# Last keys' scores beside the value products of the pairs before, row sums on another PSUM bank, and a first tile in fp32

## The chip, the cores and the metric

The kernel runs on one core of a Trainium2 chip. The metric is the device time of one execution in microseconds (us). Five engines take part: TensorE (PE; its weight loads are shown as PEld), VectorE (DVE), ScalarE (ACT), GpSimd (POOL) and the queue SP, which issues all DMAs. Each runs its own instructions in the order in which the program holds them, and waits where an instruction needs what another engine makes.

## What is computed

The reference chains three blocks over a batch of 4 with 448 positions. The inputs q and k are scaled by 8.

```python
# 1: attention with capped scores, 12 heads of 64
scores = cap * np.tanh((q @ k.T / 8) / cap)          # q, k, v: (4, 12, 448, 64), cap = 30
attn = np.exp(scores - scores.max(-1))
x = (attn / (attn.sum(-1) + 1e-9)) @ v               # heads joined: (4, 448, 768)
# 2: feed-forward with a gated convolution
h = np.maximum(x @ w_in, 0.0)                        # (4, 448, 1024)
c = conv over positions of h, 3 taps per channel
x = (h * sigmoid(c)) @ w_out                         # (4, 448, 768)
# 3: four experts of causal attention (width 64), the top two per position weighted
for e in range(4):
    q, k, v = x @ wq[e], x @ wk[e], x @ wv[e]
    out += weight[e] * (causal_softmax(q @ k.T / 8) @ v @ wo[e])
```

## The kernel before

The program is written as a list of operations (class `Plan`), each with its engine; `ORDER`, a table of numbers, then says in which order they are issued, and `SWAP` which copies stand on DVE instead of ACT or the other way round. Nothing is decided at run time.

**Block 1** works on pairs of heads, g = 0 to 23, six for each batch; rows 0 to 63 of the array hold one head of the pair and rows 64 to 127 the other. The 448 keys are three tiles of 128 keys and 64 last keys.
- `load(g)` fetches q and k. The first six pairs (`JOINT = 6`, batch 0) come as one padded block `kq` of 960 columns, in which the 64 last keys of both heads are laid out as a tile of 128 columns with zeros. Later pairs come as two transfers from `qk_more`.
- `split(g)` makes a high and a low part of q and k (type fp32r). A score is then three products: high times high, high times low, low times high.
- `qk(g, c)`: for c = 0 to 2 the scores of 128 keys, six products in 64x128 tiles, into two PSUM banks; then tanh and exp on ACT (operands called fm<-ps and fm<-fm in the profile). For c = 3 (`NK`) the last keys: in batch 0 three products of 128 rows for each pair, later, for two pairs at once, four plain fp32 products in 64x64 tiles (each fp32 product is two records) into banks 5 and 6.
- `pv(g)`: the value product in fp32, 128x64 tiles. In batch 0 eight products (sixteen records), the last keys among them; later six (twelve records), and after the second pair of a double four 64x64 products for the last keys of both. It ends in bank 7 in batch 0, later in bank 1 (even pairs) or 2 (odd pairs), from which ACT or DVE copies it (`OSB`).
- `sums(g)`: after every second pair the row sums of the exponentials, eight products in 128x32 tiles; batch 0 gathers them in bank 0 and adds four products for the last keys, later batches use bank 2, from which DVE's `gather` adds them up.
- `recip(b)` and `x_unit(b, i)`: the reciprocal of a batch's sums, spread by products and multiplied into the values, which DVE then splits.

**Block 2**: `wi_prep` decodes w_in (stored as 64-bit floats) on DVE and ACT, quarter by quarter, while batches 0 and 1 run; `f_unit(b, f, half)` is nine products of x with w_in, in 128x128 tiles. The first of them, of batch 0 (tag `f0_0`), is the point that the steps below call F. These products are the filler between the attention of the next batch. Results go to DRAM. `fold_mm` multiplies w_out with the weights of block 3, and **block 3** follows from 318 us or so to the end (`v_unit`, `proj_unit`, `scores2`, `tr2`, `pv2`, `wo_unit`).

All matrix products are recorded at line 373, transposes at 377, ACT's work at 313, DVE's at 321, DMAs at 382. A product in another tiling than the one before it (64x128, 64x64, 128x64, 128x32, 128x128) is a change of tiling.

Of the kernel before, what the change touches and what calls it, by code (L numbers as in the profile page):

```python
# [1417 lines left out]
```

## Time and profile before

| what | value |
| --- | --- |
| median of 3 runs | 539.81 us (539.22 to 539.86) |
| profiled execution | 539.78 us, its span 538.1 us |
| PE, PEld busy | 528.6 us (98%), 416.0 us (77%) |
| DVE, ACT busy | 457.4 us (85%), 364.8 us (68%) |
| chain that ended last | PE 88%, DVE 6%, ACT 4% |
| DMA | 64.03 MB, mean 119 GB/s |

An engine's busy time is the union of its instructions; a duration shown is longer than the step to the next instruction where the two overlap. The span runs from the first to the last record of the execution. A row of the timeline has a start, a duration, the engine, the operands, the number of instructions merged in it, and in brackets the idle time before it with what ended it.

### The profile page before, as it was taken

What the parts mean: (1) busy time and instruction counts of PE and PEld (TensorE: products, weight loads), DVE (VectorE), ACT (ScalarE), POOL (GpSimd) and SP (SyncE); (2) the same over time, 40 slices, a digit from 0 to 9 for tenths busy, and PEclk for the clock granted to TensorE, in tenths of its full rate; (3) what the DMA queues carried; (4) which work ended last, traced back from release to release, by engine and by line L of the source; (5) the groups of instructions that cost most, each with busy time, mean ns of one, the idle gap of its engine ahead of it and who ended that gap; (6) DMA issues with size and microseconds to landing.
All of it is one profiled execution on the core that took longest, in us unless ns stands there. A gap on an engine that the chain in (4) does not pass through costs nothing.

```text
span 538.1 us, 9349 instructions
## 1 busy us (share of the span) xinstructions
PE 528.6 (98%) x3304; PEld 416.0 (77%) x3304; DVE 457.4 (85%) x1070; ACT 364.8 (68%) x666; POOL 17.4 (3%) x71
## 2 busy tenths in 40 slices
PE   8899999999999999999999999999999999999997
PEld 6455777455656767569999999999978998999886
DVE  7999998988878886999868999798998988964772
ACT  6999967878985867943324656647857884853672
POOL 8000000000000000000000003000000000000000
PEclk9999999999999999999999999999999999999999
DMA  7464444521512251136657441245235134404413
GB/s 237 144 184 148 136 138 160 149 87 54 158 49 81 93 156 56 54 107 188 163 196 223 118 133 27 78 131 151 77 92 152 58 94 132 123 2 105 122 71 138
DMA packets 41535, 64.03 MB, mean 119 GB/s; under 512 B 7184, under 2 KB 30224, under 8 KB 41488
## 3 DMA queue, kind: packets, MB, share of 16 engines
q1 hardware_dynamic: 41488, 63.44, 39.7%
q8 instruction: 26, 0.43, 0.3%
q14 instruction: 21, 0.17, 0.1%
HBM read 41.13 MB, written 12.85 MB: 100 GB/s over the span
## 4 chain that ended last, share of the span: by engine, by line
PE 88%; DVE 6%; ACT 4%; issue 1%; DMA 1%; ACTq 0%; DVEq 0%
PE ps L373 85%; ACT fm L313 4%; DVE fm L321 3%; DVE rm L321 3%; PE ps L377 3%; DMA fm<-first 1%; ACT rm L313 0%; DVE ps L321 0%; ACTq L313 0%; DVEq L321 0%
## 5 line engine op out<-in xcount | busy, mean ns | idle before, releaser
L373 PE MATMUL ps<-rm 128*128 128x448 f32 (+5 forms) x2352 | 409.6, 352 | 2.4 <-ACT fm L313 1.3
L373 PEld LDWEIGHTS ps<-rm 128*128 128x128 f32 (+1 forms) x2352 | 357.4, 188 | 56.5 <-issue 14.7
L313 ACT ACTIVATE fm<-fm 128x448 f32<-128x448 f32 (+8 forms) x219 | 163.4, 770 | 46.8 <-DVE fm L321 35.5
L321 DVE SCALAR_TENSOR_TENSOR fm<-fm 128x448 f32<-128x448 f32 (+5 forms) x240 | 148.1, 634 | 7.0 <-ACT fm L313 4.5
L313 ACT ACTIVATE fm<-ps,fm 128x896 f32<-128x896 f32 (+4 forms) x143 | 109.9, 788 | 36.8 <-DVE fm L321 18.4
L373 PE MATMUL ps<-fm 128*64 128x448 f32 (+7 forms) x824 | 114.0, 469 | 3.2 <-ACT fm L313 1.8
L321 DVE TENSOR_TENSOR rm<-fm,rm 128x448 fp32r<-128x448 f32 (+4 forms) x152 | 89.4, 603 | 8.7 <-ACT rm L313 7.6
L373 PEld LDWEIGHTS ps<-fm 128*64 128x64 f32 (+3 forms) x824 | 44.6, 133 | 60.3 <-issue 41.4
L313 ACT ACTIVATE fm<-ps 128x448 f32<-128x448 f32 (+4 forms) x113 | 49.9, 463 | 46.3 <-PE ps L373 33.7
L321 DVE TENSOR_TENSOR fm<-fm 64x448 f32<-64x448 f32 (+6 forms) x112 | 60.7, 550 | 7.3 <-ACT fm L313 6.4
L313 ACT ACTIVATE rm<-fm 128x448 fp32r<-128x448 f32 (+6 forms) x83 | 42.7, 535 | 24.4 <-DVE fm L321 15.2
L321 DVE TENSOR_SCALAR fm<-fm 128x256 int32<-128x256 int32 (+11 forms) x138 | 43.2, 320 | 7.3 <-ACT fm L313 6.2
L321 DVE CAST rm<-fm 128x448 fp32r<-128x448 f32 (+6 forms) x77 | 30.8, 403 | 3.8 <-DMA fm<-first 2.6
L321 DVE COPY fm<-ps 128x448 f32<-128x448 f32 (+5 forms) x43 | 18.3, 433 | 12.9 <-PE ps L373 7.1
L313 ACT ACTIVATE rm<-ps 128x386 fp32r<-128x386 f32 (+3 forms) x39 | 16.1, 422 | 15.1 <-PE ps L373 12.8
L321 DVE TENSOR_REDUCE fm<-ps 128x1 f32<-128x128 f32 (+3 forms) x56 | 24.7, 448 | 0.6
L321 DVE TENSOR_TENSOR ps<-ps,fm 128x128 f32<-128x128 f32 (+1 forms) x56 | 15.3, 285 | 10.3 <-PE ps L373 8.8
L321 DVE TENSOR_TENSOR fm<-fm,ps 128x448 f32<-128x448 f32 (+1 forms) x30 | 16.5, 573 | 5.5 <-PE ps L373 5.1
L321 DVE TENSOR_TENSOR rm<-ps,rm 128x386 fp32r<-128x386 f32 (+1 forms) x32 | 18.7, 587 | 2.9 <-ACT rm L313 2.7
L396 POOL MEMSET fm<- 64x3 f32 (+12 forms) x43 | 7.2, 200 | 368.0 <-DVE fm L321 367.1
L377 PE MATMUL ps<-fm 128*128 128x128 f32 x128 | 17.4, 274 | 0.3 <-ACT fm L313 0.3
L377 PEld LDWEIGHTS ps<-fm 128*128 128x128 f32 x128 | 14.7, 140 | 1.6 <-ACT fm L313 0.5
(22 smaller groups left out, 71.6 us busy)
## 6 DMA issues: line engine op xcount, KB each, us to landing
g_dram<-fm SPq DMA_DIRECT2D x32, 224.0 KB, 3.2
fm<-g_dram SPq DMA_DIRECT2D x32, 224.0 KB, 2.9
fm<-w_in SPq DMA_DIRECT2D x24, 256.0 KB, 3.4
fm<-woT SPq DMA_DIRECT2D x16, 384.0 KB, 3.4
out<-fm SPq DMA_DIRECT2D x23, 224.0 KB, 2.3
fm<-v SPq DMA_DIRECT2D x24, 192.0 KB, 3.5
fm<-qk_more SPq DMA_DIRECT2D x18, 256.0 KB, 3.5
rm<-rm SPq DMA_DIRECT2D x32, 128.0 KB, 2.3
```

The lines of the kernel that those rows point to most:

```text
L313: return self.add("act", cost, [lambda: self.nc.scalar.activation(out, in_, func, **kw)], [out] + more, [in_] + ptr)
L321: return self.add("dve", cost, [lambda: f(out, *ins, **kw)], [out], aps)
L373: self.nc.tensor.matmul(out, a, b, start=start, stop=stop, **kw))
L377: calls = [lambda o=o, i=i, d=d: self.nc.tensor.transpose(o, i, d) for o, i, d in parts]
L396: self.add("pool", cost, [lambda: f(out, *ins, **kw)], [out], [x for x in list(ins) + [kw.get("in_")] if hasattr(x, "ap")])
```

## The change

Four things are changed together, and the whole table of issue is new.
- All 24 pairs are loaded and split alike: q with its 64 last keys (512 columns) and the 384 other keys as two transfers; `JOINT` and the padded block are gone. For the very first pair q and the first 128 keys come first, then the other keys, then the last keys.
- `last_keys(g)`: the four fp32 products for the last keys of pairs g and g + 1, their tanh and exp, in all batches, placed by their due time (`QQ_L`) beside the value products of the two pairs before; the value product of batch 0 takes the form that the later batches had, in banks 7 and 2.
- `sums` uses bank 3 instead of bank 2 in batches 1 to 3; it may be recorded ahead of later work (`sums_now`).
- The very first tile of scores (g = 0, c = 0) is two plain fp32 products of unsplit q and k instead of six products of split ones.

The diff, cut to its core; what is left out are the two tables and the data layout on the host.

```diff
-JOINT = 6
+QQ_L = 1.0
...
     def load(g):
-        if g >= JOINT:
-            RAW[g] = RQT.next(), RKT.next()
-            for t, c in zip(RAW[g], (slice(0, QS_N), slice(QS_N, QS_N + KW))):
-                pl.load(t, qk_more[g - JOINT][:, c])
+        q, k = RQT.next(), RKT.next()
+        if g:
+            RAW[g] = q[:, :S], k, q[:, S:]
+            for t, c in ((q, slice(0, QS_N)), (k, slice(QS_N, QS_N + KW))):
+                pl.load(t, kq[g][:, c])
             return
-        RAW[g] = RAWT.next()
-        if g:
-            pl.load(RAW[g], kq[g])
-        else:
-            pl.load(fm.take(1 + HEAD, raw_at - 1), first)
-            pl.load(RAW[g][:, HEAD:], kq[0][:, HEAD:])
+
+        r, n = fm.take(S + KW, raw_at), HEAD - S
+        RAW[0] = r[:, :S], r[:, S:], fm.take(KR, later + 3 * WI_C)
+        pl.load(fm.take(1 + HEAD, raw_at - 1), first)
+        pl.load(r[:, HEAD:], kq[0][:, QS_N + n:])
+        pl.load(RAW[0][2], kq[0][:, S:QS_N])
...
+    def last_keys(g):
+
+        parts, ps = [], banks[:, 5:7]
+        for i, y in enumerate((g, g + 1)):
+            q, _, k = RAW[y]
+            for j, (a, _) in enumerate(sides):
+                parts.append((ps[halves(y)[j], i, :S], k[a], q[a], True, True))
+            PS[y] = cut(P2B, 2)[:, i]
+        pl.mm(parts)
+        p = cut(P2B, 2)
+        pl.act(p, ps[:, :, :S], AF.Tanh, scale=tsc)
+        pl.act(p, p, AF.Exp, scale=cap_in)
...
-        f = 1 if c == 2 and g >= JOINT else (3, 5, 1)[(4 * g + c) % 3] if g < NP else 3 + 2 * (c % 2)
+        f = (3, 5, 1)[c]
...
+        if g == c == 0:
+            parts = [(o, RAW[0][1][a, :128], RAW[0][0][a], True, True) for o, a in lanes]
...
-        if not whole and g >= JOINT:
-
-            if not g % 2:
-                return
-            parts, ps = [], banks[:, 5:7]
-            for i, y in enumerate((g - 1, g)):
-                r = RAW.pop(y)[0]
-                for j, (a, _) in enumerate(sides):
-                    parts.append((ps[halves(y)[j], i, :S], r[a, S:], r[a, :S], True, True))
-            pl.mm(parts)
...
     def pv(g):
-        ps = PB[g % 2] if g >= JOINT else bank(7)
+        ps = PB[g % 2] if g >= NP else bank((7, 2)[g % 2])
         O[g] = ps
-        gs = (g,) if g < JOINT else (g - 1, g) if g % 2 else ()
+        gs = (g - 1, g) if g % 2 else ()
...
-        more, sb = b in DIRECT, bank(2 if b else 0)
+        more, sb = b in DIRECT, bank(3 if b else 0)
...
             if g < NG:
+                if g % 2 == 0 and s == (2 if g else NK):
+                    at(q - QQ_L, "qq%d_%d" % divmod(g, NP))
+                    last_keys(g)
```

What the new order makes of this is shown at three places. First TensorE at the very start. In these rows the size is that of the output; ps<-fm 128x128 are idle products that keep the engine at work, ps<-rm the products of split parts, ps<-fm 64x448 value products and 64x64 groups, one row for each product. Before:

```order
L373 MATMUL ps<-fm 128x128 x7
L373 MATMUL ps<-rm 128x448 x12
L373 MATMUL ps<-fm 128x128
L373 MATMUL ps<-rm 128x448 x3
L373 MATMUL ps<-fm 128x128 x3
L373 MATMUL ps<-rm 128x448 x6
L373 MATMUL ps<-fm 128x128
L373 MATMUL ps<-rm 128x448 x21
L373 MATMUL ps<-fm 64x448 x8
```

The same place after the change, up to the first value products:

```order
L374 MATMUL ps<-fm 128x128 x5
L374 MATMUL ps<-fm 128x448 x2
L374 MATMUL ps<-rm 128x448 x12
L374 MATMUL ps<-fm 128x128 x5
L374 MATMUL ps<-fm 64x448 x4
L374 MATMUL ps<-fm 128x128
L374 MATMUL ps<-rm 128x448 x6
L374 MATMUL ps<-fm 128x128
L374 MATMUL ps<-rm 128x448 x24
L374 MATMUL ps<-fm 64x448 x20
```

The two plain products of the first tile stand ahead of all split ones, the last keys of the first two pairs among the idle products, and the value products of two pairs in one run of twenty with a group of last keys.

Second, TensorE in batch 1, around the row sums (32x224) of its second and third double. Before:

```order
L373 MATMUL ps<-fm 64x448 x12
L373 MATMUL ps<-rm 128x448 x12
L373 MATMUL ps<-fm 64x448 x4
L373 MATMUL ps<-fm 32x224 x8
L373 MATMUL ps<-fm 64x448 x4
L373 MATMUL ps<-rm 128x448 x33
L373 MATMUL ps<-fm 64x448 x16
L373 MATMUL ps<-fm 32x224 x8
L373 MATMUL ps<-rm 128x448 x15
```

The same stretch after the change:

```order
L374 MATMUL ps<-fm 64x448 x20
L374 MATMUL ps<-fm 32x224 x8
L374 MATMUL ps<-rm 128x448 x54
L374 MATMUL ps<-fm 64x448 x12
L374 MATMUL ps<-fm 32x224 x8
L374 MATMUL ps<-fm 64x448 x8
L374 MATMUL ps<-rm 128x448 x15
```

The last keys (x4 on their own before) stand in one run with the value products and their shared part, and scores no longer stand between them.

Third, VectorE from the reciprocal of batch 0's sums on, the way to F. ps in an operand is a product that is read from PSUM, rm a split part that is written; 128x256 is w_in. Before:

```order
L321 RECIPROCAL fm<-ps 128x224
L321 SCALAR_TENSOR_TENSOR fm<-fm 128x256
L321 CAST rm<-fm 128x224
L321 SCALAR_TENSOR_TENSOR rm<-rm,fm 128x224
L321 SCALAR_TENSOR_TENSOR fm<-fm 128x256
L321 TENSOR_TENSOR rm<-fm,rm 128x256
L321 TENSOR_TENSOR fm<-fm,ps 128x448 x2
L321 CAST rm<-fm 128x448
L321 TENSOR_TENSOR fm<-fm,ps 128x448
L321 CAST rm<-fm 128x448
L321 TENSOR_TENSOR fm<-fm,ps 128x448
L321 TENSOR_TENSOR rm<-fm,rm 128x256
```

After the change:

```order
L322 RECIPROCAL fm<-ps 128x224
L322 TENSOR_TENSOR rm<-fm,rm 128x448 x2
L322 CAST rm<-fm 128x224
L322 TENSOR_TENSOR rm<-fm,rm 128x256
L322 SCALAR_TENSOR_TENSOR rm<-rm,fm 128x224
L322 SCALAR_TENSOR_TENSOR fm<-fm 128x256
L322 TENSOR_SCALAR fm<-fm 128x256
L322 TENSOR_TENSOR fm<-fm,ps 128x448 x2
L322 SCALAR_TENSOR_TENSOR fm<-fm 128x256 x3
L322 TENSOR_TENSOR fm<-fm,ps 128x448 x2
L322 SCALAR_TENSOR_TENSOR fm<-fm 128x896
L322 CAST rm<-fm 128x448
```

Between the reciprocal and the split that F needs stand more decoding of w_in, two splits of the next pairs' q and a sum over 896 columns. Up to that split they are 33 instructions, where 19 stood before.

## Rows read from the trace of the kernel before

**Rows 1.** Page: the span, and the engines' busy time, share and instructions.

```profile
span 538.1 us, 9349 instructions
PE 528.6 (98%) x3304; PEld 416.0 (77%) x3304; DVE 457.4 (85%) x1070; ACT 364.8 (68%) x666; POOL 17.4 (3%) x71
```

**Rows 2.** Stretches: length, busy time of each engine, granted clock, DMA share, GB/s.

```profile
0.00:57.00 57.00, 53.65 (x370) 30.37 (x370) 52.92 (x115) 51.51 (x58) 12.93 (x57) 1.00 0.56 173
57.00:126.00 69.00, 67.29 (x440) 44.51 (x436) 62.65 (x136) 53.27 (x72) 0.00 (x0) 1.00 0.41 126
126.00:340.00 214.00, 214.00 (x1301) 167.42 (x1294) 186.66 (x346) 137.11 (x201) 4.35 (x12) 1.00 0.39 117
```

**Rows 3.** Timeline of TensorE at F, the first product with w_in.

```profile
59.92 0.47 PE L373 MATMUL ps<-rm 128*128 128x448 f32 x1
```

**Rows 4.** TensorE's waits (us, times, longest), and its timeline at two row sums.

```profile
PE ps L373 <- ACT fm L313: 3.1, 6, 1.1
...
PE ps L373 <- DMA fm<-v: 0.3, 1, 0.3
...
103.11 1.88 PE L373 MATMUL ps<-fm 128*32 128x224 f32 x24 [0.75 <-ACT fm L313]
...
116.11 1.15 PE L373 MATMUL ps<-fm 128*32 128x224 f32 x16 [0.69 <-ACT fm L313]
```

**Rows 5.** Timeline of TensorE in batch 0: last keys, row sums, a value product.

```profile
35.95 0.86 PE L373 MATMUL ps<-rm 128*128 128x448 f32 x3
36.75 3.98 PE L373 MATMUL ps<-fm 128*64 128x224 f32 x24
...
42.88 3.23 PE L373 MATMUL ps<-fm 128*64 128x448 f32 x16
```

**Rows 6.** Timeline of TensorE in batches 1 to 3: steps with and without changes.

```profile
78.30 2.09 PE L373 MATMUL ps<-rm 128*128 128x448 f32 x9
80.31 0.61 PE L373 MATMUL ps<-fm 64*64 64x448 f32 x4
...
139.90 0.98 PE L373 MATMUL ps<-fm 64*64 64x448 f32 x8
140.81 5.12 PE L373 MATMUL ps<-rm 64*128 64x448 f32 x26
...
261.89 18.40 PE L373 MATMUL ps<-rm 128*128 128x448 f32 x90
```

**Rows 7.** Timelines of TensorE and ScalarE in the opening, and ScalarE ahead of F.

```profile
1.11 3.35 PE L373 MATMUL ps<-fm 128*128 128x128 f32 x14 [1.11 <-DVE fm L577]
...
8.34 0.83 PE L373 MATMUL ps<-fm 128*128 128x128 f32 x6
...
6.57 2.60 ACT L313 ACTIVATE fm<-ps,fm 128x896 f32<-128x896 f32 x3 [0.53 <-PE ps L373]
...
58.16 0.58 ACT L313 ACTIVATE rm<-fm 128x448 fp32r<-128x448 f32 x1
```

**Rows 8.** Groups by form, TensorE: count, busy us, mean ns of one, idle before.

```profile
L373 PE MATMUL ps<-fm 64*64 64x448 f32 x144 | 17.5, 560 | 0.4 <-ACT fm L313 0.4
```

**Rows 9.** Timeline of VectorE from 38 us to F.

```profile
38.42 1.15 DVE L321 SCALAR_TENSOR_TENSOR fm<-fm 128x896 f32<-128x896 f32 x1
...
49.46 0.28 DVE L321 TENSOR_SCALAR fm<-fm 128x256 f32<-128x256 f32 x1
49.66 0.41 DVE L321 SCALAR_TENSOR_TENSOR fm<-fm 128x256 int32<-128x256 int32 x1
...
50.73 1.55 DVE L321 RECIPROCAL fm<-ps 128x224 f32<-128x224 f32 x1
...
56.31 0.62 DVE L321 TENSOR_TENSOR fm<-fm,ps 128x448 f32<-128x448 f32 x1
56.84 0.42 DVE L321 TENSOR_TENSOR rm<-fm,rm 128x256 fp32r<-128x256 f32 x1
...
59.28 0.62 DVE L321 TENSOR_TENSOR rm<-fm,rm 128x448 fp32r<-128x448 f32 x1
```

More of the change, by code (lines that the diff above doesn't have):

```diff
@@ L27 @@
 SG = S + 64
-KQ = S + SG
 QS_N = S + KR
@@ L56 @@
 LV_0 = 4
+WI_C = 256
 WI_0 = 0.5
@@ L453, with chain_kernel @@
 F_WORDS = 19712
-def chain_kernel(tc, first, kq, qk_more, v, w_in, conv_w, woT, wqkv, wo, out):
+def chain_kernel(tc, first, kq, v, w_in, conv_w, woT, wqkv, wo, out):
     nc = tc.nc
@@ L504, in chain_kernel @@
     cap_in, eps, tsc = capt[:, 63:], capt[:, 4:5], capt[:, 5:6]
-    RAWT = fm.ring(2, KQ)
-    fm.take(3 * QS_N + 2 * KW - 2 * KQ)
+    fm.take(3 * QS_N + 2 * KW)
     RQT = Ring([fm.take(QS_N, raw_at + n) for n in (0, QS_N + 2 * KW, 2 * QS_N + 2 * KW)])
@@ L528, in chain_kernel @@
     RC, one_1 = rm.take(SH), tri[:, :96]
-    ZT = rm.ring(3, 2 * KQ)
+    ZT = rm.ring(3, 2 * (S + KW))
     bank = lambda i: banks[:, i]
@@ L555, in split @@
     def split(g):
-        if g >= JOINT:
-            z, rs = ZT.next(), [t[:, :n] for t, n in zip(RAW[g], (S, KW))]
-            KQ_H[g], KQ_L[g] = z[:, :KQ], z[:, KQ:]
-            cs = slice(0, S), slice(S, S + KW)
-            for i in range(2):
-                pl.pick(i == 0, KQ_H[g][:, cs[i]], rs[i])
-            for i in range(2):
-                pl.tt(KQ_L[g][:, cs[i]], rs[i], f32(KQ_H[g][:, cs[i]]), OP.subtract)
-            return
-        r, z = RAW.pop(g), ZT.next()
-        h, l = KQ_H[g], KQ_L[g] = z[:, :KQ], z[:, KQ:]
-        parts = (slice(0, S), slice(S, HEAD), slice(HEAD, KQ)) if g == 0 else (slice(0, KQ),)
-        for i, c in enumerate(parts):
-            pl.pick(i % 2 == 0, h[:, c], r[:, c])
-        for c in parts:
-            pl.tt(l[:, c], r[:, c], f32(h[:, c]), OP.subtract)
+        z, (q, k, _) = ZT.next(), RAW[g]
+        h, l = KQ_H[g], KQ_L[g] = z[:, :S + KW], z[:, S + KW:]
+        cs = [(q, slice(0, S))] + [(k[:, n:m], slice(S + n, S + m)) for n, m in (((0, 128), (128, KW)) if g == 0 else ((0, KW),))]
+        for i, (r, c) in enumerate(cs):
+            pl.pick(i % 2 == 0, h[:, c], r)
+        for r, c in cs:
+            pl.tt(l[:, c], r, f32(h[:, c]), OP.subtract)
     at(-100, "st")
@@ L636, in chain_kernel @@
     pl.ts(eps, capt[:, 2:3], 1e-9 / 128, None, OP.mult)
-    P, S2, O, OSB = {}, {}, {}, {}
-    held = []
+    P, PS, S2, O, OSB = {}, {}, {}, {}, {}
+    held, sums_due = [], []
     PB = [bank(1), bank(2)]
+    def last_keys(g):
[9 more added lines that the diff above has]
+        pl.act(p, p, AF.Exp, scale=cap_in)
     def qk(g, c):
@@ L646, in qk @@
         if c == 2:
-            if g < JOINT:
-                P[g][1] = cut(P1T[g % 2], 3)
-            else:
-                P[g][1] = cut(P2A[g % 2 if g < P_3 else (g - P_3 + 2) % 3], 2)
-        if c == NK:
-            P[g].append(P[g][1][:, 2] if g < JOINT else cut(P2B, 2)[:, g % 2])
-        whole = c < NK
-        f = 1 if c == 2 and g >= JOINT else (3, 5, 1)[(4 * g + c) % 3] if g < NP else 3 + 2 * (c % 2)
+            P[g][1] = cut(P2A[g % 2 if g < P_3 else (g - P_3 + 2) % 3], 2)
+        f = (3, 5, 1)[c]
         ps = banks[:, f:f + 2]
@@ L657, in qk @@
         h, l = KQ_H[g], KQ_L[g]
-        lanes = [(ps[:, j, :S], a) for j, (a, _) in enumerate(sides)] if whole else [(ps[:, 0, :S], slice(0, 128))]
+        lanes = [(ps[:, j, :S], a) for j, (a, _) in enumerate(sides)]
         parts = [(o, u[a, k], w[a, x], i == 0, i == 2) for i, (u, w) in enumerate(((h, h), (h, l), (l, h)))
                  for o, a in lanes]
+        if g == c == 0:
+            parts = [(o, RAW[0][1][a, :128], RAW[0][0][a], True, True) for o, a in lanes]
         step = len(lanes) if g == 0 and c < 2 else len(parts)
@@ L670, in qk @@
             step = len(parts)
-        if not whole and g >= JOINT:
-            if not g % 2:
-                return
-            parts, ps = [], banks[:, 5:7]
-            for i, y in enumerate((g - 1, g)):
-                r = RAW.pop(y)[0]
-                for j, (a, _) in enumerate(sides):
-                    parts.append((ps[halves(y)[j], i, :S], r[a, S:], r[a, :S], True, True))
-            pl.mm(parts)
-            p = cut(P2B, 2)
-            pl.act(p, ps[:, :, :S], AF.Tanh, scale=tsc)
-            pl.act(p, p, AF.Exp, scale=cap_in)
-            for y in (g - 1, g):
-                add_shared(y)
-            return
         for i in range(0, len(parts), step):
@@ L694, in qk @@
             pl.act(P[g][0], P[g][0], AF.Exp, scale=cap_in)
+            place = pl.pos, pl.bias, pl.kind
+            sums_now()
+            pl.pos, pl.bias, pl.kind = place
             S2[g] = cut(S2T.next(), 2)
@@ L697, in qk @@
             return
-        n = 2 if whole else 1
         p = P[g][c // 2]
-        q = slice(2 * (c % 2), 2 * (c % 2) + n)
-        pl.act(p[:, q], ps[:, :n, :S], AF.Tanh, scale=tsc)
-        if c % 2 or c == 2 and g >= JOINT:
+        q = slice(2 * (c % 2), 2 * (c % 2) + 2)
+        pl.act(p[:, q], ps[:, :, :S], AF.Tanh, scale=tsc)
+        if c:
             pl.act(p, p, AF.Exp, scale=cap_in)
@@ L706, in qk @@
             pl.stt(S2[g], p[:, 0:2], eps, p[:, 2:4], OP.add, OP.add)
-        if c == (NK if g < JOINT else 2) and g // NP not in WHOLE:
+        if c == 2 and g // NP not in WHOLE:
             pl.tt(S2[g], S2[g], p[:, 0:2], OP.add)
-        if c == NK:
+        if c == 2:
             add_shared(g)
@@ L714, in add_shared @@
             for j, a in enumerate(halves(g)):
-                pl.tt(S2[g][a, j], S2[g][a, j], P[g][2][a], OP.add)
+                pl.tt(S2[g][a, j], S2[g][a, j], PS[g][a], OP.add)
     def pv(g):
-        ps = PB[g % 2] if g >= JOINT else bank(7)
+        ps = PB[g % 2] if g >= NP else bank((7, 2)[g % 2])
         O[g] = ps
-        gs = (g,) if g < JOINT else (g - 1, g) if g % 2 else ()
-        parts = [(ps[a, :S], VT[g][c // NK][:, 2 * (c % NK) + j], P[g][c // 2][:, 2 * (c % 2) + j] if c < NK else P[g][2], c == 0, c == NK)
-                 for c in range(NK + (g < JOINT)) for j, (a, _) in enumerate(sides)]
+        gs = (g - 1, g) if g % 2 else ()
+        parts = [(ps[a, :S], VT[g][c // NK][:, 2 * (c % NK) + j], P[g][c // 2][:, 2 * (c % 2) + j], c == 0, False)
+                 for c in range(NK) for j, (a, _) in enumerate(sides)]
         pl.mm(parts)
-        if g >= JOINT:
-            parts = []
-            for x in gs:
-                for j, (a, _) in enumerate(sides):
-                    k = halves(x)[j]
-                    parts.append((O[x][a, :S], VT[x][1][k, j], P[x][2][k], False, True))
-            if parts:
-                pl.mm(parts)
+        parts = []
+        for x in gs:
+            for j, (a, _) in enumerate(sides):
+                k = halves(x)[j]
+                parts.append((O[x][a, :S], VT[x][1][k, j], PS[x][k], False, True))
+        if parts:
+            pl.mm(parts)
         for x in gs:
@@ L757, in sums @@
         r = p // 2
-        first, last = (r == 0, r == 2) if b < JOINT // NP else (True, True)
-        more, sb = b in DIRECT, bank(2 if b else 0)
+        first, last = (r == 0, r == 2) if b < 1 else (True, True)
+        more, sb = b in DIRECT, bank(3 if b else 0)
         for t in range(1 + (b in WHOLE)):
@@ L763, in sums @@
         if more:
-            pl.mm([(sb[a, :SH], one_s[c][:, i, r], P[g - 1 + i][2][:, SH * c:SH * c + SH], False, last and c == 1)
+            pl.mm([(sb[a, :SH], one_s[c][:, i, r], PS[g - 1 + i][:, SH * c:SH * c + SH], False, last and c == 1)
                    for c in range(2) for i, (a, _) in enumerate(sides)])
-        if b >= JOINT // NP:
+        if b >= 1:
             gather(g, sb)
     def recip(b):
-        if b < JOINT // NP:
+        if b < 1:
             r = ET.next()[:, :SH]
@@ L891, in conv_gate, with sums_now @@
         pl.stt(c, c, 1.0, e, OP.add, OP.mult)
+    def sums_now():
+        while sums_due:
+            (b, p), pos = divmod(sums_due[0][0], NP), sums_due[0][1]
+            at(pos, "sm%d_%d" % (b, p))
+            sums(sums_due.pop()[0])
+            if p == NP - 1:
+                at(pos, "x%d" % b)
+                recip(b)
     NG = B * NP
@@ L899, in chain_kernel @@
             if s == 0:
-                for x in (g - 1,) if 1 <= g <= JOINT else (g - 2, g - 1) if JOINT < g <= NG and not g % 2 else ():
+                for x in (g - 2, g - 1) if 0 < g <= NG and not g % 2 else ():
                     at(q + PV_L, "pv%d_%d" % divmod(x, NP))
@@ L909, in chain_kernel @@
                             f_unit(b - 1, u // 2, u % 2, G2, q + F_0[b - 1] + F_S[b - 1] * u, FP_L)
-                if g + 2 < NG and (g % 2 == 0 or g < JOINT):
-                    at(q - LD_L, "ld%d_%d" % (b, p))
-                    load(g + 2)
-                for x in (g + 1,) if g <= JOINT else (g, g + 1) if not g % 2 and g < NG else ():
+                for x in (1,) if not g else (g, g + 1) if not g % 2 and g < NG else ():
                     at(q + LV_0, "lv%d_%d" % divmod(x - 1, NP))
@@ L916, in chain_kernel @@
                 if g >= 2 and g % 2 == 0 and g <= NG:
-                    at(q - SM_L, "sm%d_%d" % divmod(g - 1, NP))
-                    sums(g - 1)
-                    if p == 0 and b >= 1:
-                        at(q - SM_L, "x%d" % (b - 1))
-                        recip(b - 1)
+                    sums_due.append((g - 1, q - SM_L))
+                    if g <= NP or g == NG:
+                        sums_now()
             if g < NG:
+                if g % 2 == 0 and s == (2 if g else NK):
+                    at(q - QQ_L, "qq%d_%d" % divmod(g, NP))
+                    last_keys(g)
                 at(q, "qk%d_%d" % divmod(g, NP))
-                qk(g, s)
-                if s == NK and g % 2 and JOINT < g < NG - 2:
-                    at(4 * g - LD_L, "ld%d_%d" % (b, p))
-                    load(g + 2)
+                if s < NK:
+                    qk(g, s)
+                for i in range(2):
+                    if g % 2 == 0 and s == (2 if g else NK) and g < NG - 2:
+                        at(4 * (g + i) - LD_L, "ld%d_%d" % divmod(g + i, NP))
+                        load(g + 2 + i)
             if q < 4 * ND:
@@ L1381 @@
     kh = heads(k)
-    keys = np.zeros((B, NP, 2 * D, SG), k.dtype)
-    keys[:, :, :, :S - KR] = kh[:, :, :, :S - KR]
     vp = v.reshape(B, NP, 2, S, D)
@@ L1390 @@
             h = j ^ i
-            keys[:, i::2, D * j:D * j + D, S - KR * (1 - h):S + KR * h] = kh[:, i::2, D * j:D * j + D, S - KR:]
             shared[:, i::2, h, :, j] = vp[:, i::2, j, S - KR:]
     shared = shared.reshape(B, NP, 128, 2, D)
-    kq = np.concatenate([heads(q), keys], 3)
-    qk_more = np.concatenate([heads(q), kh[:, :, :, S - KR:], kh[:, :, :, :S - KR]], 3).reshape(B * NP, 2 * D, 2 * S)[JOINT:]
+    kq = np.concatenate([heads(q), kh[:, :, :, S - KR:], kh[:, :, :, :S - KR]], 3).reshape(B * NP, 2 * D, 2 * S)
     arrays = {
-        "first": np.concatenate([np.full((2 * D, 1), cap, kq.dtype), kq[0, 0, :, :HEAD]], 1),
-        "kq": kq.reshape(B * NP, 2 * D, KQ)[:JOINT],
-        "qk_more": qk_more,
+        "first": np.concatenate([np.full((2 * D, 1), cap, kq.dtype), kq[0, :, :S], kq[0, :, QS_N:QS_N + HEAD - S]], 1),
+        "kq": kq,
         "v": np.concatenate([whole, shared], 3).reshape(B, NP, 128, NB * D),
```

2 lines of the change are left out of this document (1 added, 1 removed), and 217 rows, old and new, of tables (ORDER, SWAP).

## The prediction

> **What bounds the kernel now.** I read the shares of the engines first, then the stretches, then TensorE's waits, and last single steps on TensorE (PE) and VectorE (DVE). PE is busy for 528.6 of 538.1 us [rows 1], at a granted clock of 1.00 in every stretch [rows 2], so the first question is how much PE work the change takes away. The stretches say where that counts. From 126 to 340 us PE has no idle time at all, and there a microsecond of PE work is a microsecond of the kernel. In the first 57 us PE, DVE and ScalarE (ACT) are all busy for 90% and more [rows 2]; there less work on PE helps only if the other two don't come later. I cut the program at F, the first product with w_in, which starts at 59.92 us [rows 3]. After F PE is the bound but for short waits for ACT; of all its waits for ACT (3.1 us, six times) two of 0.75 and 0.69 us stand in front of groups of row sums [rows 4].
>
> **What goes from PE.** Steps are taken from start to start. In batch 0 the last keys' scores are six groups of three products with 128 rows, 0.80 us each with the two changes of tiling around them [rows 5]; they become three groups of 64x64 tiles, as the later batches have them already, eight records in 0.91 us with their changes [rows 6]. The value products of batch 0 lose four of their sixteen records (3.23 us for sixteen [rows 5], 3.0 without the changes around them, so 0.75 us for four) and get three groups of eight 64x64 records. Without the changes of tiling this is 6 x 0.61 - 3 x 0.75 = 1.4 and 6 x 0.75 - 3 x 0.75 = 2.25 us less. The first tile in fp32 is not in the trace as a form: two lanes side by side, which take 0.75 us at the rate of the other fp32 products, or up to 1.5 us if it still runs as the fourteen opening records do (3.35 us for fourteen against 0.83 for six [rows 7]); the six records that it replaces cost 0.61. Together some 3.5 us less, all of it ahead of F.
>
> **Changes of tiling.** Nine products with w_in that stand alone take 80.31 - 78.30 = 2.01 us; in a long run 90 records take 18.4 us, which is 1.82 for nine [rows 6]. So a change in and one out cost 0.19 us together, for the 64x64 groups 0.15; a change-over has one of each, and I take 0.18. Counted in the two orders, PE changes its tiling 123 times before and 104 times after: 29 and 33 times ahead of F, 94 and 71 times behind it. Behind F that is 23 x 0.18 = 4.1 us (3.5 at 0.15). If PE alone decided, the kernel would gain 3.5 + 19 x 0.18 = 6.9 us.
>
> Four 64x64 products of such a group write two banks, each bank from two row halves of the array. In the trace 144 such records, 560 ns each, are busy for 17.5 us in all [rows 8], so four and more run at a time. The Trainium skill, "TensorEngine Tiling (Array Packing)", section "Gotcha 1: PSUM Pressure", says that different row tiles cannot access one PSUM bank at the same time; by that the groups would take twice as long, and the six new ones in batch 0 would give back 6 x 0.75 = 4.5 us. The trace speaks against it.
>
> **What moves ahead of F.** The new order puts two whole value products, their shared part, one group of last keys and twelve score products (2.25 + 0.75 + 0.75 + 1.22 us, 5.0 in all) in front of F where they stood behind it. By PE's own work F would come at 59.9 + 5.0 - 3.5 + 4 x 0.18 = 62.1 us. But F waits for DVE: the last split that it needs ends at 59.28 + 0.62 = 59.90, and F starts at 59.92 [rows 3, 9]. DVE is busy from its first work on. Up to the reciprocal of batch 0 (50.73 us [rows 9]) its order holds the same work within 0.2 us. From there to the split that F waits for, the new order has 14 instructions more: five 256-wide scalar-tensor-tensors (0.34 each), three 256-wide tensor-scalars (0.20), a 256-wide tensor-tensor (0.34), three 448-wide tensor-tensors (0.53), one 896-wide scalar-tensor-tensor (1.06) and a 256-wide cast (0.20), 1.7 + 0.6 + 0.34 + 1.6 + 1.06 + 0.2 = 5.5 us; the durations are those shown less the 0.08 by which the next one overlaps [rows 9]. So F moves to 59.9 - 0.2 + 5.5 = 65.2 us, 5.3 later. ACT's last part in front of F ended at 58.16 + 0.58 = 58.7 us [rows 7]. It gets seven more instructions ahead of F, about 0.87 each [rows 7], 6.1 us, and starts some 1.3 us earlier because the first tile no longer waits for splits (first tanh at 6.57 us [rows 7]): 63.5 us, 1.7 ahead of DVE. The earlier start is therefore worth nothing here: its cover is DVE's work, and with that gone it would be worth its 1.3 us.
>
> **Behind F.** The 5.0 us that moved are gone from there, and so are 4.1 us of changes: 9.1 us. The row sums go to bank 3. In the order before they go to bank 2, which the odd value product has just filled and ACT must copy out; the waits of 0.75 and 0.69 us [rows 4] are that, and they go: 1.4 us. What is late next there: scores of the next pair go to banks 3 to 6 and now wait until DVE has gathered the sums out of bank 3, with one score group of 0.8 us in between, in seven places; and last keys' tanh must have left banks 5 and 6 by then. The trace has no such wait. Its bounds are nothing (the gather ends in time) and one DVE instruction in front of each gather, 7 x 0.5 = 3.5 us. I take 0.4 us, nearer to nothing, since DVE idles here (62.65 of 69.00 us busy [rows 2]).
>
> **DMA and the queue.** q and k of batch 0 come as two transfers for each pair instead of one, and the last keys of the first pair as a small third one: six more issues on SP. The first large load of values falls from the 7th to the 13th place, behind loads that wait for PE and DVE. PE waited 0.3 us for values once [rows 4]; it may now be 0 to 1 us, ahead of F, and DVE covers it.
>
> **The sum.** 5.3 - 9.1 - 1.4 + 0.4 = -4.8 us. The profiled execution took 539.78 us, 1.7 over its span, and the median of the runs is 539.81, so both give 535.0 us. About 0.2% (1.1 us) is what a measurement can tell from no change.
>
> **Rivals.** (a) PE sets F after all: DVE is freed earlier than its count says, as its casts were slow (1 us and less) while the opening ran. Then F comes at 62.1, 3.1 us sooner: 531.9 us. For it speaks that DVE lost 4.1 us in the opening stretch [rows 2]; against it that those losses come from the first transfer, which stays. (b) The gathers and the copies of the last keys come late in all seven places and at the split of batch 1, whose DVE order leaves little room: 3 us more, 538 us. For it: only 0.8 us of PE work stand between. Against: before, sums and gather followed one another without such waits. (c) Slower: in batch 0 the value products of both pairs now stand back to back, so PE waits for the second pair's exponentials while ACT waits for the scores queued behind them. It costs at each of the four doubles (three in batch 0, one at the first of batch 1) what ACT has then to wait. ACT has its lead of 1.7 us on DVE, so it is hidden up to about 0.4 us a double; to eat the gain of 4.8 it must reach (4.8 + 1.7) / 4 = 1.6 us each, two tanh instructions. At 2.2 us each the time is 542. Against it: other score products stand between most of them. (d) The change doesn't do what it says: the changes of tiling were hidden by the loads of weights, and the 4.1 us don't come: 539.1 us. Against it stand the 2.01 and 1.82 us. (e) The new 64x64 groups of batch 0 take turns at their banks: 4.5 us back, 539.5 us; the 17.5 us speak against it, and the skill's section named above for it.
>
> **How the numbers follow.** The forecast of 535.0 (533 to 537 as the gathers and the price of a change-over go) 0.60, (a) 0.15, (b) 0.13, (c) 0.05, (d) 0.05, (e) 0.02. The range reaches from (a) to (b): 531.5 to 538.2. Faster by over 0.2% (below 538.7): the forecast, (a) and most of (b), 0.87; within 0.2%: (d), (e) and the rest of (b), 0.08; slower: (c), 0.05.
>
> **What would show it.** F at 64.5 to 66 us, started by DVE: the step on DVE is right; at 62, (a). Behind F no wait of PE for ACT in front of the row sums. In batches 1 to 3 the value products, their shared part and the last keys in one run of 20 fp32 calls, without gaps. PE waiting for DVE right behind the row sums, at 0.3 us and more each: (b). ACT idle by 2 us and more between 12 and 45 us, with PE waiting for ACT in front of value products: (c). Time after 340 us should be as before. The forecast is wrong if F comes after 67, or if PE idles by over 3 us in all between F and 130 us.

## The result, and the profile after

The changed kernel takes 535.40 us (median of 4 runs, 534.79 to 536.08) where the kernel before took 539.84 beside it (median of 4, 539.22 to 541.19). The ratio is 0.9915, with a 95% interval of 0.9893 to 0.9937, so it is faster by 3.4 to 5.8 us. The forecast was 535.0 in a range of 531.5 to 538.2. Measured again later (e12 below) the same kernel took 534.86 us (median of 6) beside 539.95 for the kernel before.

The head of the page of the changed kernel stands against [rows 1]: the span is 5.0 us shorter, and TensorE's (PE's) busy time 4.7 us.

```profile
span 533.1 us, 9365 instructions
PE 523.9 (98%) x3308; PEld 414.7 (78%) x3308; DVE 455.5 (85%) x1080; ACT 367.8 (69%) x666; POOL 16.9 (3%) x71
```

Where the 5.0 us went is read best with the stretches cut at the points that the prediction uses: up to F (the first product with w_in), from F to the first product of block 3, and block 3. The columns are those of [rows 2]. First the kernel before:

```profile
0.00:59.90 59.90, 56.55 (x386) 31.44 (x386) 55.82 (x122) 54.41 (x61) 12.93 (x57) 1.00 0.55 171
59.90:335.00 275.10, 273.39 (x1675) 206.00 (x1674) 241.83 (x465) 183.96 (x260) 4.35 (x12) 1.00 0.40 121
335.00:538.10 203.10, 198.63 (x1247) 178.52 (x1245) 159.71 (x486) 126.46 (x347) 0.15 (x2) 1.00 0.36 101
```

The same three stretches of the changed kernel:

```profile
0.00:64.60 64.60, 61.27 (x430) 30.73 (x430) 60.19 (x146) 59.81 (x68) 12.58 (x56) 1.00 0.53 169
64.60:330.70 266.10, 264.82 (x1636) 205.40 (x1633) 230.79 (x435) 187.32 (x266) 3.21 (x11) 1.00 0.40 121
330.70:533.10 202.40, 197.81 (x1248) 178.60 (x1246) 164.54 (x500) 120.66 (x333) 1.16 (x5) 1.00 0.37 102
```

F comes 4.7 us later (5.3 were forecast). The long middle is 9.0 us shorter (10.1 forecast): PE's busy time there falls by 8.6 us and its idle time from 1.7 to 1.3 us. Block 3 is 0.7 us shorter (no change forecast). 4.7 - 9.0 - 0.7 = -5.0 us.

PE's waits over the whole span answer to the first line of [rows 4], where ACT (ScalarE) had 3.1 us. Then PE's timeline around two groups of row sums (the records in 128x32 tiles, drawn together with the products in front of them where nothing but the shape changes), and between them the first value product of batch 2.

```profile
PE ps L374 <- ACT fm L314: 2.6, 6, 0.9
...
PE ps L374 <- DVE fm L322: 0.6, 2, 0.4
...
84.12 0.96 PE L374 MATMUL ps<-fm 128*32 128x224 f32 x16
85.02 0.88 PE L374 MATMUL ps<-rm 64*128 64x448 f32 x6
86.26 6.82 PE L374 MATMUL ps<-rm 64*128 64x448 f32 x42 [0.36 <-DVE fm L322]
...
124.65 2.48 PE L374 MATMUL ps<-fm 128*64 128x448 f32 x12 [0.88 <-ACT fm L314]
...
145.57 7.39 PE L374 MATMUL ps<-fm 128*64 128x448 f32 x56
```

The waits in front of row sums (0.75 and 0.69 us in [rows 4]) are gone. The row at 145.57 us is one run of 56 records without a gap: two value products, their shared part, the last keys of the next two pairs and the row sums. Two waits are new: scores at 86.26 us wait 0.36 us for the gather by VectorE (DVE), and the first value product of batch 2 waits 0.88 us for ACT.

How PE and DVE come to F stands in the next rows: PE at four places ahead of it, then DVE's last split that F's nine products need.

```profile
25.27 2.11 PE L374 MATMUL ps<-rm 64*128 64x448 f32 x18
...
31.09 2.48 PE L374 MATMUL ps<-fm 128*64 128x448 f32 x12 [0.50 <-ACT fm L314]
...
40.42 0.88 PE L374 MATMUL ps<-rm 64*128 64x448 f32 x6 [0.56 <-ACT fm L314]
...
51.52 2.25 PE L374 MATMUL ps<-rm 64*128 64x448 f32 x18
53.99 0.92 PE L374 MATMUL ps<-rm 64*128 64x224 f32 x8 [0.22 <-ACT fm L314]
55.16 3.21 PE L374 MATMUL ps<-rm 64*128 64x448 f32 x22 [0.24 <-DVE fm L322]
58.29 6.39 PE L374 MATMUL ps<-fm 128*64 128x448 f32 x40
64.62 0.47 PE L374 MATMUL ps<-rm 128*128 128x448 f32 x1
...
64.45 0.62 DVE L322 TENSOR_TENSOR rm<-fm,rm 128x448 fp32r<-128x448 f32 x1
```

The split ends at 65.07 us; 65.2 was forecast. But F does not wait for it: PE goes from the value products into F without a gap at 64.62 us, and only the last of F's nine products need that split. The kernel before shows the same in the row right in front of the one in [rows 3]:

```profile
57.52 2.48 PE L373 MATMUL ps<-fm 128*64 128x448 f32 x12
```

Twelve such records take 2.41 us from start to start in the changed kernel too (the row at 27.31 us, which nothing holds), so PE came to F at 59.92 us without a gap. So the number was right, and whether DVE sets it was open. This is what most experiments below ask.

### The profile page after: what moved, and what is told of

The parts are those of the page before. It is cut to its first block, busy times and chain, and to the rows that moved or that the text cites. A ratio compares the mean times of both kernels' runs of the same rounds, so it can differ in the third digit from the quotient of the medians.

```text
span 533.1 us, 9365 instructions
## 1 busy us (share of the span) xinstructions
PE 523.9 (98%) x3308; PEld 414.7 (78%) x3308; DVE 455.5 (85%) x1080; ACT 367.8 (69%) x666; POOL 16.9 (3%) x71
## 4 chain that ended last, share of the span: by engine, by line
PE 82%; DVE 14%; issue 1%; ACT 1%; DMA 1%; SPq 0%; DVEq 0%
PE ps L374 80%; DVE fm L322 9%; DVE rm L322 5%; PE ps L378 2%; DMA fm<-w_in 1%; ACT fm L314 1%; ACT rm L314 0%; SPq L383 0%; DVEq L322 0%
## 5 line engine op out<-in xcount | busy, mean ns | idle before, releaser
L374 PE MATMUL ps<-rm 128*128 128x448 f32 (+5 forms) x2328 | 403.9, 352 | 2.8 <-ACT fm L314 1.2
L314 ACT ACTIVATE fm<-fm 128x448 f32<-128x448 f32 (+7 forms) x222 | 164.0, 766 | 46.1 <-DVE fm L322 27.5
L322 DVE SCALAR_TENSOR_TENSOR fm<-fm 128x448 f32<-128x448 f32 (+4 forms) x240 | 147.4, 631 | 10.6 <-ACT fm L314 8.8
L374 PE MATMUL ps<-fm 64*64 64x448 f32 (+7 forms) x852 | 114.2, 472 | 2.6 <-ACT fm L314 1.4
L314 ACT ACTIVATE fm<-ps 128x448 f32<-128x448 f32 (+5 forms) x110 | 48.8, 464 | 35.0 <-PE ps L374 23.4
L314 ACT ACTIVATE rm<-fm 128x448 fp32r<-128x448 f32 (+7 forms) x91 | 46.8, 536 | 29.5 <-DVE fm L322 25.1
L322 DVE TENSOR_SCALAR fm<-fm 128x256 f32<-128x256 f32 (+9 forms) x138 | 42.0, 319 | 8.4 <-ACT fm L314 7.0
L322 DVE CAST rm<-fm 128x448 fp32r<-128x448 f32 (+5 forms) x74 | 27.0, 369 | 1.5 <-PE ps L374 1.3
L322 DVE COPY fm<-ps 128x448 f32<-128x448 f32 (+5 forms) x47 | 20.4, 442 | 7.0 <-PE ps L374 3.3
L322 DVE TENSOR_REDUCE fm<-ps 128x1 f32<-128x256 f32 (+3 forms) x56 | 24.4, 447 | 0.6
```

The costliest lines, as they stand in the source:

```text
L314: return self.add("act", cost, [lambda: self.nc.scalar.activation(out, in_, func, **kw)], [out] + more, [in_] + ptr)
L322: return self.add("dve", cost, [lambda: f(out, *ins, **kw)], [out], aps)
L374: self.nc.tensor.matmul(out, a, b, start=start, stop=stop, **kw))
```

## The experiments

The profiles of the changed kernel and of those whose opening is the same put F at 64.62, 64.54, 64.29 and 64.33 us. Shifts of F below 0.3 us therefore mean nothing. Times are medians; the changed kernel's is 535.40 us, and 534.86 in e12. The kernel before, measured beside the experiments, took 540.08 (e1 to e4), 540.27 (e5 to e8), 540.31 (e9 and e10) and 539.95 us (e11 and e12), so half a microsecond between two experiments means little.

**The first tile in split parts again (e1).** The very first tile of scores is made of six products as in the kernel before; the order is otherwise kept.

```diff
-        if g == c == 0:
-            parts = [(o, RAW[0][1][a, :128], RAW[0][0][a], True, True) for o, a in lanes]
```

> The changed kernel, but its very first tile of scores is six products of split parts again (the two plain fp32 products are gone); all else keeps its order. My theory: ScalarE's first tanh comes some 1 to 1.3 us later, but F (first product with w_in) is set by VectorE's last split (65.07 us), so F stays at 64.6 +- 0.3 us and the time within 0.3 us of the changed kernel's 535.4. Rival: the opening is one chain in which a later start of ScalarE moves everything behind it; then F comes at 65.6 to 66 us and the time is 536.4 to 536.8 us.

The time was 535.71 us. ACT's first tanh, and F, first as changed and then in this run:

```profile
5.54 3.02 ACT L314 ACTIVATE fm<-ps,fm 128x896 f32<-128x896 f32 x3 [0.58 <-PE ps L374]
```

```profile
7.29 2.81 ACT L315 ACTIVATE fm<-ps,fm 128x896 f32<-128x896 f32 x3 [2.33 <-PE ps L375]
...
65.38 0.47 PE L375 MATMUL ps<-rm 128*128 128x448 f32 x1
```

The tanh is 1.75 us later, F 0.8 to 1.1 us. The time is 0.3 us above the changed kernel's, or 0.85 above that of e12; against the kernel before, e1 gains 4.4 us where the changed kernel gains 4.4 and 5.1. So the early start is worth something, between the two theories: about half of it reaches F, and 0.1 to 0.7 us show in the time, hardly more than the spread.

**Row sums on bank 2 (e2).** One line; besides, products of the order were put behind a copy or a gather where bank 2 now asks for it.

```diff
-        more, sb = b in DIRECT, bank(3 if b else 0)
+        more, sb = b in DIRECT, bank(2 if b else 0)
```

> The changed kernel, but the row sums of batches 1 to 3 go to bank 2 as before; the order is kept except where a product has then to come behind a copy or a gather. My theory: each of the nine groups of row sums waits for the copy of the odd value product, 0.7 us each as in the two places of the kernel before (0.75 and 0.69 us), 6.3 us in all: 541.7 us or, where scores that use bank 2 are pushed back too, more. Rival: the bank does not matter (the waits of before came from elsewhere): 535.4 +- 0.5 us.

547.25 us in one run, 11.9 us more. PE's waits for ACT and for DVE (3.1 us more are for splits), and two of its places:

```profile
PE ps L374 <- ACT fm L314: 4.6, 10, 1.1
PE ps L374 <- DVE fm L322: 3.3, 7, 1.6
...
86.20 0.87 PE L374 MATMUL ps<-rm 64*128 64x448 f32 x5 [1.59 <-DVE fm L322]
88.16 7.38 PE L374 MATMUL ps<-rm 64*128 64x448 f32 x48 [1.10 <-ACT fm L314]
```

More than the 6.3 us of the theory, but not in the way it said: of the nine groups of row sums only two show a wait in front of them (0.23 us at 102 us, 0.67 us at 209 us). The scores of every pair's third tile go to banks 1 and 2, so they now wait for the gather (the row at 86.20 us stands right behind row sums), and more waits for ACT and DVE follow. Part of the 11.9 us is the order that had to give way; the two were not separated. So in the new order bank 2 costs far more than the 1.4 us of waits of the old order, and that those two waits were for the copy of the odd value product is not shown by this run.

**Sixteen changes of tiling more (e3).** The same work, neighbours exchanged at eight places between 131 and 240 us. PE's order around 220 to 235 us, where nine products in 128x128 tiles go between value products:

```diff
-MATMUL ps<-rm 128x448 x60
-MATMUL ps<-fm 64x448 x16
+MATMUL ps<-rm 128x448 x51
+MATMUL ps<-fm 64x448 x6
+MATMUL ps<-rm 128x448 x9
+MATMUL ps<-fm 64x448 x10
```

> The changed kernel with the same work, but at eight places between 131 and 240 us two neighbouring products of different tilings stand in exchanged order, so that TensorE changes its tiling 120 times instead of 104. My theory (a change-over costs 0.18 us and TensorE is the bound there): 16 x 0.18 = 2.9 us more, 538.3 us, with no new waits. Rival (the change is hidden by the loads of weights): 535.4 +- 0.5 us.

538.70 us, 3.3 us more than the changed kernel and 3.8 more than e12. The profile of e12 is the one to compare with, since the first exchanged product stands at the same place in both (137.25 and 137.26 us). The rows are the stretch with all sixteen changes, and behind it 180 products whose order is the same in both kernels. This run, then e12:

```profile
137.25:246.24 108.99, 108.99 (x693) 71.47 (x689) 87.50 (x144) 83.15 (x104) 0.00 (x0) 1.00 0.29 90
246.24:283.54 37.30, 37.30 (x182) 33.90 (x181) 29.03 (x58) 11.11 (x22) 0.00 (x0) 1.00 0.68 204
```

```profile
137.26:243.18 105.92, 105.92 (x694) 72.40 (x690) 86.91 (x143) 82.84 (x103) 0.00 (x0) 1.00 0.29 91
243.18:279.75 36.57, 36.57 (x182) 33.90 (x181) 29.44 (x59) 11.39 (x22) 0.00 (x0) 1.00 0.70 212
```

The stretch with the changes is 3.07 us longer, 0.19 us for each of sixteen, all of it in PE's busy time. That is the forecast's 0.18. The other 0.73 us come behind it, where no order was changed: there a product takes 0.207 instead of 0.203 us at a granted clock of 1.00 in both, and why is open. From 283.54 and 279.75 us on the two take the same time (253.06 and 253.05 us), and no wait of PE between 126 and 340 us is shown in either. So the changes are paid in full where PE is the bound. At the other seven places products in 64x128 tiles (scores, at one place those that spread the sums) are exchanged with products in 128x128 tiles; what a change costs for each pair of tilings was not separated. The Trainium skill, "TensorEngine Tiling (Array Packing)", section "Key Properties", says that changing the tiling mode drains TensorE. It gives no price; this run has one.

**The third quarter of w_in decoded later (e4).** Order alone: eight DVE instructions (2.3 us) and three of ACT go behind the last split for F.

> The changed kernel, but eight VectorE instructions (2.3 us) and three of ScalarE that decode the third quarter of w_in stand behind VectorE's last split for F instead of ahead of it. My theory (VectorE's last split sets F): the split ends at 62.8 us and F comes at 62.3 to 62.8 us instead of 64.62; the time falls by up to 2 us, to 533.5, unless the products with the third quarter (80.4 us) then wait for it. Rival: F is set by TensorE's own queue and its earlier waits; F moves by less than 0.5 us, and the time does not fall.

540.90 us, 5.5 us more. DVE's last split for F, and PE at F and behind it:

```profile
62.31 0.62 DVE L322 TENSOR_TENSOR rm<-fm,rm 128x448 fp32r<-128x448 f32 x1
...
57.69 6.39 PE L374 MATMUL ps<-fm 128*64 128x448 f32 x40
64.01 3.98 PE L374 MATMUL ps<-rm 128*128 128x448 f32 x18
69.22 0.47 PE L374 MATMUL ps<-rm 128*128 128x448 f32 x1 [1.23 <-ACT rm L314]
70.04 0.88 PE L374 MATMUL ps<-rm 128*128 128x448 f32 x3 [0.36 <-DVE rm L322]
73.16 17.12 PE L374 MATMUL ps<-rm 128*128 128x448 f32 x74 [2.24 <-DVE rm L322]
```

The split ends at 62.93 us, 2.1 us sooner, and F moves by 0.3 to 0.6 us only: it starts 1.1 us after the split, right behind the value products. So the last split does not release F. The price comes behind F: the products with w_in then wait for ACT and DVE, 3.8 us in three places. The rest is the clock, which stands in front of the last two columns (those of [rows 2]):

```profile
68.00:73.16 5.16, 1.35 (x4) 0.67 (x4) 4.26 (x12) 3.70 (x9) 0.00 (x0) 0.77 0.29 102
73.16:77.66 4.50, 4.50 (x12) 4.02 (x13) 4.28 (x9) 1.68 (x4) 0.00 (x0) 0.50 0.62 211
```

PE is busy for 1.35 of the 5.16 us from 68.00 us on. Then it works for 4.50 us at a granted clock of 0.50 (1.2 GHz), until the clock is 1.00 (2.4 GHz) again: some 2.2 us of work are lost (an estimate, half of 4.50). With the 3.8 us of waits that is 6.1 us, as much as the 5.5 us and the 0.3 to 0.6 us by which F came sooner. The changed kernel has no such stretch. The decoding was not in the way ahead of F; it was due.

**One exp left out (e5), one sum left out (e6).** e5 leaves out ACT's exp of the first 256 keys of the fourth pair, e6 DVE's sum over 896 columns for the first pair of batch 1; both outputs lack that part.

```diff
-        if c:
+        if c and (g, c) != (3, 1):
             pl.act(p, p, AF.Exp, scale=cap_in)
```

```diff
+            if g != NP:
-            pl.stt(S2[g], P[g][0][:, 0:2], eps, P[g][0][:, 2:4], OP.add, OP.add)
+                pl.stt(S2[g], P[g][0][:, 0:2], eps, P[g][0][:, 2:4], OP.add, OP.add)
```

> The changed kernel without one exp of ScalarE in batch 0, that of the first 256 keys of the fourth pair (1.8 us at 29.26 us), which the value product at 31.09 us waits for; its softmax weights are left as the capped scores. Theory now (before F ScalarE sets the pace of batch 0, and VectorE stands 0.4 to 0.6 us behind it): the wait of 0.50 us at 31.09 goes, F comes 0.5 to 1 us sooner (63.6 to 64.1 us) and the time falls by as much, to 534.5 to 534.9. Rival (VectorE's last split alone sets F, as predicted): F stays at 64.3 to 64.6 and the time at 535.4.

> The changed kernel without one VectorE instruction between the reciprocal and the last split for F: the sum over 896 columns for the first pair of batch 1 (1.06 us at 57.74 us); its row sums lack those keys. Prediction's step (VectorE's last split sets F): the split ends at 64.0 instead of 65.07, F comes up to 1 us sooner and the time falls to 534.4. Theory now (TensorE's own queue brings F at 64.6, VectorE's split is as late but not alone): F moves by 0.2 us at most, the time by less than 0.3.

e5 took 535.0 us, e6 534.45. PE in e5 where the exp is missing, then F:

```profile
30.26 2.48 PE L375 MATMUL ps<-fm 128*64 128x448 f32 x12
...
33.71 0.67 PE L375 MATMUL ps<-rm 64*128 64x448 f32 x4 [0.57 <-DVE rm L323]
...
64.38 1.29 PE L375 MATMUL ps<-rm 128*128 128x448 f32 x5
```

In e6, DVE's last split for F, F, and the place behind the row sums at 84 us:

```profile
63.51 0.62 DVE L323 TENSOR_TENSOR rm<-fm,rm 128x448 fp32r<-128x448 f32 x1
...
64.58 1.28 PE L375 MATMUL ps<-rm 128*128 128x448 f32 x5
...
84.01 0.96 PE L375 MATMUL ps<-fm 128*32 128x224 f32 x16
84.91 3.33 PE L375 MATMUL ps<-rm 64*128 64x448 f32 x23
```

e5: the value product no longer waits 0.50 us for ACT (it starts at 30.26 instead of 31.09 us), but two products further on PE waits 0.57 us for DVE, and F stays. The theory that ACT alone sets the pace ahead of F falls as the one on DVE did. e6: F stays, as expected, and the split is early again (64.13 us). But the wait of 0.36 us for the gather at 86 us is gone: DVE's 1.06 us counted there, behind F. The time is 0.4 us below that of e12 and 0.95 below the changed kernel's first, so the "less than 0.3" that I expected was too small.

**Other orders of the same work (e7 to e11).** These kernels hold the changed kernel's operations on the same engines and banks; only the order table differs, so no diff is shown. e12 is the changed kernel once more.

> The changed kernel with the same operations on the same engines and banks, only in another order on all engines up to the end, chosen so that TensorE's waits shrink: 105 changes of tiling instead of 104. Theory (TensorE's work cannot shrink further without other changes, but its waits of 0.50, 0.56, 0.4 and 0.88 us at 31, 40, 86 and 125 us and the many short ones ahead of F can): 2.5 to 5 us less, 530.5 to 533. Rival (the three engines are all full ahead of 126 us, so a wait removed comes back elsewhere): 535.4 +- 0.7 us.

> A second order of the same kind as the run before (103 changes of tiling): with the same theory 530.5 to 533 us, with the rival 535.4 +- 0.7 us; the two orders agree within 0.7 us if it is the waits and not a lucky place.

> The changed kernel with the same operations on the same engines and banks in another order, as in the two orders before it, but now everything up to the first row sums (some 20 us), all DMAs and all of GpSimd's work keep their places, and ahead of F few VectorE instructions stand right behind the one whose result they read (those steps took 0.12 to 0.13 us longer in every trace, and the two slow orders had them two to three times as often). Theory (TensorE's waits of 0.5, 0.56, 0.36 and 0.88 us at 31, 40, 86 and 125 us and the short ones can be emptied by order alone): F at 64 us or sooner, 531.5 to 533.5 us. Rival (they come back elsewhere): 535.4 +- 0.5 us, or slower as the two orders before.

> As the run before, with fewer instructions moved. Theory: 532.5 to 534.5 us, F within 0.3 us of the changed kernel's 64.62, the gain behind F. Rival: 535.4 +- 0.5 us.

> The changed kernel with the order of the run before (e10) up to the first product of batch 1 with w_in (132 us) and its own order behind it. There e10 had lost 1.5 us in two waits at 151 and 174 us, and ahead of it gained 0.6 us, the wait for the gather at 86 us above all. Theory: the gather's wait is gone without a new one, so 0.3 to 0.8 us less than the changed kernel in the same call. Rival (the gain ahead is spread of the opening only): no difference, within 0.3 us.

> The changed kernel itself once more, as a measure for the run before and of how far F moves from one profile to the next: 535.4 us +- 0.5, F at 64.3 to 64.7 us.

Measured: e7 558.16 and e8 553.16 us; e9 536.93, e10 535.70, e11 534.66, e12 534.86. None beats the changed kernel: e11 is 0.2 us below e12, which is no difference, though its wait at 86 us is gone (F came 0.5 us later). For e7 to e9 the theories failed, and the rivals' 535.4 us did not come either. e10 shows the pattern: between F and 132 us it gains 0.6 us on the changed kernel, and between 151 and 199 us it loses 1.5, with a wait of 0.97 us for ACT at 177 us.

Why e7 is 22.8 us slower is seen in part on DVE, which is full ahead of F (F came at 72.84 us) but gets less done. A cast of e7 and the split behind it, then the same form of cast in the changed kernel and what stands behind it there:

```profile
32.57 0.36 DVE L322 CAST rm<-fm 128x384 fp32r<-128x384 f32 x1
32.96 0.56 DVE L322 TENSOR_TENSOR rm<-fm,rm 128x384 fp32r<-128x384 f32 x1
```

```profile
30.14 0.35 DVE L322 CAST rm<-fm 128x384 fp32r<-128x384 f32 x1
30.41 0.42 DVE L322 SCALAR_TENSOR_TENSOR fm<-fm 128x256 int32<-128x256 int32 x1
```

The split reads the cast's result, and the step from one start to the other is 0.39 us; where something else stands between, it is 0.27. Over the whole of e7 the next instruction starts 0.034 us (median) after the end of one whose result it reads, and 0.083 us before the end of any other that it follows without a wait. In the order of e7 DVE has 403 such neighbours, in the changed kernel 154, in e9 302; DVE's busy time for the same 1080 instructions is 473.7, 455.5 and 465.7 us. What counts is where they stand: ahead of F e7 has 71, the changed kernel and e9 17 each. At 0.12 us the 54 more are 6.5 of the 8.2 us by which F comes later (an estimate). e9 has its 148 more behind F, and is 1.5 to 2.1 us slower in all.

The clock is a second cause. Right ahead of F in e7, then in e9:

```profile
59.00:62.60 3.60, 1.01 (x9) 0.73 (x9) 3.36 (x6) 3.09 (x4) 0.00 (x0) 1.00 0.92 299
62.60:66.00 3.40, 3.36 (x19) 2.81 (x20) 3.33 (x7) 1.62 (x2) 0.00 (x0) 0.50 0.63 216
```

```profile
53.00:56.50 3.50, 2.39 (x20) 1.27 (x16) 3.47 (x10) 3.50 (x6) 0.00 (x0) 1.00 0.44 128
56.50:59.90 3.40, 3.40 (x18) 2.74 (x20) 3.17 (x8) 3.40 (x4) 0.00 (x0) 0.50 0.84 260
```

In both PE had idled, for 2.6 and 1.1 us of the stretch before, and then worked for 3.4 us at a granted clock of 0.50: some 1.7 us lost (an estimate, half of 3.4). In e9 that is about as much as its F (65.95 us) comes later than the changed kernel's. e8 had 6.8 and 3.4 us at 0.50. What e7 loses behind F, some 14.6 us, was not explained, and the two causes were not tested apart.

## Why the prediction was right, and where it was not

**The sum.** -4.8 us was forecast; the span fell by 5.0 and the median by 4.4. The terms are off by up to 1.1 us, in both directions, and the 5.3 us for F, of which 4.7 came, stand on a step that failed (below): that this term came out is luck.

**What bounds the kernel, and the price of changes.** Right. Behind F PE's busy time in the middle stretch fell by 8.6 us, where 9.1 were expected (5.0 moved ahead of F and 4.1 for 23 changes of tiling). e3 shows from the other side that changes cost their full price there, 0.19 us each where 0.18 was forecast, so rival (d) falls. The new groups of 64x64 tiles do not take turns at their banks:

```profile
L374 PE MATMUL ps<-fm 64*64 64x448 f32 x192 | 21.3, 551 | 0.0
```

With 192 records instead of 144 the mean is 551 ns, before 560 [rows 8], and 192 x 0.551 = 106 us of records keep PE busy for 21.3 us; rival (e) falls. The rule of the Trainium skill that the prediction quoted for it ("TensorEngine Tiling (Array Packing)", section "Gotcha 1: PSUM Pressure") does not hold for these groups.

**F by DVE's last split.** The time was right, 65.07 us for the split and 64.62 for F, but the step is wrong: e4 and e6 brought the split 2.1 and 0.9 us forward and F did not follow by more than 0.6. What delays F beyond the 62.1 us that were counted for PE alone are, as far as the rows show it, short waits for ACT and DVE strewn from 20 to 58 us, of which only a part is shown as idle. Between 51.52 and 58.29 us PE runs 36 records of scores and 12 of the x products. Eighteen score records take 2.04 us from start to start where nothing holds them (the row at 25.27 us; the next one starts at 27.31), so 36 take some 4.1 and the 12 others, which are half as wide, 0.9 at two thirds of that: 5.0 us (an estimate). They take 6.8, with 0.46 us shown as idle. That all of the delay is of this kind was not shown. e5 shows what kind of bound this is: take a wait for ACT away, and the next is one for DVE. Three engines that are busy for 93 to 95% of the stretch release one another, and less work on one of them moves F by 0 to 0.6 us. That DVE's count landed within 0.15 us of its split is no luck, since it was busy all the way. That F came with it is: the prediction took a coincidence in [rows 3, 9] (59.90 and 59.92) for a cause, where PE's own row at 57.52 us, shown above, ran into F without a gap.

**The earlier start "worth nothing".** Wrong by its size: e1 puts it at 0.8 to 1.1 us of F and 0.1 to 0.7 us of time. The reason given, that DVE covers it, went with the step above.

**Bank 3.** The 1.4 us of the two waits went, as said, and the gather was late once by 0.36 us instead of in all seven places: 0.4 was forecast, and rival (b) falls. That the two waits came from bank 2 fits this, but was not shown apart (e2 had other waits). What the list of what is late next lacked is the 0.88 us for ACT at the first value product of batch 2. So waits fell by 0.4 us in the middle stretch and not by 1.0.

**Block 3.** "As before" was wrong by 0.7 us. Its products are the same, but they stand in another order there too, as the whole table is new. PE's busy time fell from 198.63 to 197.81 us, and its idle time did not (4.5, then 4.6 us). Why was not tested.

**Rivals (a) and (c).** F at 62.1 us did not come. For (c) a value product at 31 us waits 0.50 us for ACT, so the mechanism exists, at a third of the price from which it would have decided; the 0.56 us at 40 us stand in front of scores.

## What to carry to other kernels

Where one engine has no idle time, count its work and its changes of mode, and the result follows: 9.1 us were counted here and 8.6 found. Where several engines are full at once, don't look for the one event that releases the next stage: an experiment that takes work from one engine tells whether it counts, and for F here none did alone. When an order is changed to remove waits, look at what then stands side by side on a full engine, and at the granted clock: in e4, e7 and e9 PE lost more than its waits. When an added cost is measured, take it from the stretch that was changed: the whole span of e3 would have given 0.24 us a change, the stretch gives 0.19.
